# A branchformer forward and backward kernel: local steps paced by a VectorE budget, row scalings on ScalarE, conv weight gradient as tap products on TensorE

## The chip, the cores and the metric

One Trainium2 chip, one core of it. The metric is the device time of one execution, in microseconds, median over the runs of a job. A ratio is the mean time of one kernel's fast runs over that of the other's fast runs of the same rounds, so it is not quite the ratio of the medians quoted.

Words used throughout:

- A **unit** is a 1000-column piece of one 128-row block of the attention matrix. It has two **places** at which other work is put in. Four units are one row block, so eight places. A place is about 1.9 us here.
- The **local steps** are the work of the conv branch (GELU, layernorm, depthwise conv, their gradients), done for a **pair** of row blocks at a time and strewn over the places.
- A **conv** is the `pc` product group of a pair. Its channels 128 to 143 come as 80 rows (5 taps x 16 channels) through DRAM: a store to `gnC_d` (or `dgC_d` in the backward conv), then a load. This load is called the **gnC load** (or dgC load).

## The reference

```python
def _fwd_reference(x, w_qkv, w_att_out, w_mlp_in, dw_csgu, w_mlp_out, dw_merge, w_merge):
    B, T, D = x.shape                      # 2, 4000, 144; bf16; K = 5 taps
    xa = _layernorm(x)
    q, k, v = split(xa @ w_qkv)
    p = _softmax(q @ k.T * D ** -0.5)
    glob = (p @ v) @ w_att_out
    h = _gelu(xa @ w_mlp_in)
    u, g = h[..., :D], _layernorm(h[..., D:])
    gc = depthwise_conv(g, dw_csgu)        # gc[t] = sum_i g[t+i-2] * dw_csgu[i]
    loc = (u * gc) @ w_mlp_out
    m = concat(glob, loc);  m = m + depthwise_conv(m, dw_merge)
    return x + m @ w_merge
# the kernel returns this output and the gradients of all eight inputs for a given grad_out
```

The part that the change rebuilds is the gradient of `dw_csgu`: for each tap and channel, the sum over all tokens of `g` shifted by the tap, times the gradient that arrives at `gc`.

## The kernel before

For each of the two sequences there is a head, an attention stage with the local steps inside it, and a tail. The code of the attention stage that the change and the argument touch (cuts marked `# ...`):

```python
class Steps:                               # strews generators over the places
    def place(self, tensor=True):
        # all 'V' steps that are due (VectorE, ScalarE, GpSimd, DMA), as many as are ready
        # ... then at most one 'P' step (TensorE)

def pair(p):                               # local steps of row blocks 2p, 2p+1
    # ... GELU and layernorm give h_, gn, rs
    yield 'P', 2, aft(("gn", 1), ("ug", 2), ("wg", 4))
    gnC.put(p, gn)                         # 4 transposes, copies by ScalarE, store of 16 rows to gnC_d
    # ...
    yield 'V', 2                           # two places later
    gnC.fill(p)                            # the gnC load of pair p-1: 80 rows
    yield 'P', 4, ((("gn", min(p + 1, NPR - 1)), 6),) + aft(("ug", 1))   # four places after its load at the earliest
    pc = gnC.conv(p, False)                # last product of each block reads the 80 rows (w_c)
    # ... then the same with dgc through dgC.put, dgC.fill, dgC.conv

def wgrad(p):                              # gradient of dw_csgu, on VectorE
    yield 'V', 2, ((("dg", p), 2),)
    dgC.taps.spread(d8[0:80, :], p * 256, 256)
    for m in range(5):
        yield 'V', 1
        nc.vector.scalar_tensor_tensor(jg[:], a_[:, m:m + 256], 1.0, d_[:, 2:258], op0=ALU.mult, op1=ALU.mult, accum_out=dws[:, p, m:m + 1])
    # ... and one more for the 80 rows
for p in range(NPR):
    Q.add(14 * p, pair(p))
    Q.add(14 * p + 20, wgrad(p))

def row_end(i):                            # VectorE: sums, reciprocal rl, and
    nc.vector.tensor_scalar(Qs[:, pb, :], S.Q_t[:, i, :], rl[:], None, op0=ALU.mult)
    nc.vector.tensor_scalar(br[:], S.B_t[:, i, :], rl[:], None, op0=ALU.mult)
    nc.vector.scalar_tensor_tensor(Bt[:, pb, :], Qs[:, pb, :], nd[:], br[:], op0=ALU.mult, op1=ALU.add)

# a unit: pS and pD products; ScalarE: P = exp(pS); VectorE: Sm = pD * P; then
# y products (16 per unit) and X products (12 per fill); X is added into acc by VectorE, or ScalarE and GpSimd
ps_x = ps_f = Banks(pool, 3)               # three PSUM banks, shared by X and by all local steps
# all loads, stores and DMA transposes (PT, ST) of the stage are issued on SyncE's queue, in program order
```

## Time and profile before

| | before |
|---|---|
| time, median (lowest to highest), four runs | 1316.7 us (1311.2 to 1318.7) |
| profiled execution | 1318.5 us |
| TensorE / VectorE / ScalarE / GpSimd busy | 1222.5 / 986.3 / 806.0 / 580.4 us |
| the two attention stages, first `pS` to last `X` | 512.8 + 509.4 us |

The engines' line of the page of the kernel before:

```profile
PE 1222.5 (93%) x15116; PEld 957.1 (73%) x15116; DVE 986.3 (75%) x3421; ACT 806.0 (61%) x2370; POOL 580.4 (44%) x1033
```

The windows view of the kernel before, for its two attention stages (columns: the stretch, its length, busy time of each engine with the number of instructions, the granted TensorE clock, the mean busy share of the DMA engines, GB/s):

```profile
66.00:579.00 513.00, 489.55 (x5897) 369.71 (x5897) 407.62 (x1351) 328.51 (x986) 221.14 (x358) 0.99 0.87 152
...
696.00:1206.00 510.00, 488.36 (x5902) 369.56 (x5901) 407.60 (x1349) 328.37 (x987) 221.45 (x359) 0.99 0.88 151
```

TensorE is busy for 95% of these stages. That alone doesn't say that it streams at its peak. This case shows it in a striking way: the busy share is 93% before and 92% after a change that costs 35 us. So I read the distances between the starts of products. The timeline of the kernel before, TensorE:

```profile
401.09 1.16 PE L1903 MATMUL y<-ra,ST 128*128 128x144 bf16 x16
402.09 0.23 PE L1925 MATMUL X<-Qs,Sm 128*128 128x144 bf16 x1
```

Sixteen products of 144 columns take 1.00 us from start to start, 62.5 ns each. Products of 288 columns start 122 ns apart and those of 144 columns 62 ns (medians), so a column takes an estimated 0.416 ns, from these two, and some 2.5 ns a product are left. (Products of 128 columns start 56 ns apart, as this gives; those of 500 columns 215 ns, 4 ns more.) I used this as the time that a product needs and worked out, for every pair of successive products in the attention stages, what the distance holds beyond it. The rest goes to the wait that the profile names, or to a half-clock window (granted clock 0.5 in the record) if it lies in one, or to "small" (mostly a fixed 0.1 us where the array changes between 16-row and 128-row products: a 16-row product starts 158 ns after one of 144 columns, another of 144 columns 62 ns after it, medians):

| us, both attention stages | before | after |
|---|---|---|
| streaming, without the new products | 896.3 | 891.4 |
| the new tap products (`pw`) | - | 19.6 |
| small | 63.6 | 66.0 |
| waits for VectorE | 31.9 | 4.9 |
| waits for DMA | 10.8 | 40.0 |
| waits for ScalarE | 12.4 | 17.9 |
| lost to half clock | 7.2 | 23.6 |
| sum | 1022.2 | 1063.4 |

The waits of the whole kernel before, from the list of waits, TensorE (who waited for whom: us in all, times, longest):

```profile
PE X L1925 <- DVE acc L1939: 14.8, 16, 2.8
PE pc L1574 <- DMA gnC<-gnC_d: 9.1, 8, 2.1
...
PE pD L1854 <- DVE Sm L1868: 7.4, 26, 0.7
```

The groups that the change removes or moves, from the groups of the kernel before (busy us, mean ns | idle before):

```profile
L1785 DVE SCALAR_TENSOR_TENSOR jg<-gnC,dgC 128x256 bf16<-128x256 bf16 x160 | 92.0, 575 | 1.3
...
L1889 DVE TENSOR_SCALAR br<-B_t,rl 128x144 f32<-128x144 bf16 x64 | 18.5, 288 | 0.0
L1787 DVE SCALAR_TENSOR_TENSOR jg<-gnC,d 80x256 bf16<-80x256 bf16 x32 | 17.4, 545 | 0.0
L1887 DVE TENSOR_SCALAR Qs<-Q_t,rl 128x144 bf16<-128x144 bf16 x64 | 16.3, 254 | 0.0
```

### The profile page before, as it was taken

The numbers are of one execution on the slowest core, as the hardware profiler recorded it, in microseconds if no ns is written. First come the engines' busy times: TensorE is split into PE (matmuls) and PEld (weight loads), VectorE is DVE, ScalarE is ACT, GpSimd is POOL, SyncE is SP. The second block draws the span as 40 slices with busy tenths as digits, with TensorE's granted clock in tenths as the row PEclk, the third lists the DMA queues.
The fourth block names the chain that finished last, engine by engine and source line by source line (L and its number), as shares of the span: only waits on it lengthen the run. The fifth ranks groups of instructions, "written<-read, shape, count | busy, mean of one in ns | idle before, by whom it ended". The sixth has DMA issues, their size and how long they took to land. (4 is left out here: it accounts for less than half of the span.)

```text
span 1318.5 us, 39927 instructions
## 1 busy us (share of the span) xinstructions
PE 1222.5 (93%) x15116; PEld 957.1 (73%) x15116; DVE 986.3 (75%) x3421; ACT 806.0 (61%) x2370; POOL 580.4 (44%) x1033
## 2 busy tenths in 40 slices
PE   4899999999999999999989999999999999999986
PEld 2657776777777777798976677677777777779884
DVE  4666777887989888847735688788798888884664
ACT  2666666667667666546646666666766766654542
POOL 6312445444545454247611244545444544425640
PEclk9999999999999999999999999999999999999999
DMA  6369888887899889987775989888999988998851
GB/s 182 97 126 152 149 153 147 147 149 150 154 164 155 157 141 170 157 190 206 200 218 104 157 145 168 146 146 146 149 152 159 164 151 146 165 159 191 240 151 32
DMA packets 634223, 205.51 MB, mean 156 GB/s; under 512 B 577183, under 2 KB 631556, under 8 KB 633988
## 3 DMA queue, kind: packets, MB, share of 16 engines
q1 hardware_dynamic: 627472, 197.54, 79.3%
q10 hardware_dynamic: 6548, 5.33, 1.8%
q8 instruction: 120, 1.97, 0.6%
q14 instruction: 83, 0.68, 0.2%
HBM read 46.22 MB, written 21.79 MB: 52 GB/s over the span
## 5 line engine op out<-in xcount | busy, mean ns | idle before, releaser
L1868 DVE SCALAR_TENSOR_TENSOR Sm<-pD,Pm 128x500 bf16<-128x500 f32 x512 | 325.6, 673 | 104.0 <-PE pD L1858 71.4
L1866 ACT ACTIVATE Pm<-pS 128x500 bf16<-128x500 f32 x512 | 295.4, 584 | 99.6 <-PE pS L1858 96.8
L1925 PE MATMUL X<-Qs,Sm 128*128 128x144 bf16 x2048 | 286.5, 226 | 15.3 <-DVE acc L1939 14.8
L1937 POOL TENSOR_TENSOR acc<-xs,acc 128x432 f32<-128x432 f32 x150 | 172.3, 1148 | 268.3 <-ACT xs L1936 267.9
L1926 PE MATMUL X<-Bt,Pm 128*128 128x144 bf16 x2048 | 286.4, 226 | 0.8 <-DVE Bt L1890 0.8
L1926 PEld LDWEIGHTS <-Pm 128*128 128x128 bf16 x2048 | 200.6, 98 | 19.4 <-issue 18.4
L1925 PEld LDWEIGHTS <-Sm 128*128 128x128 bf16 x2048 | 200.5, 98 | 2.2 <-issue 1.0
L1903 PEld LDWEIGHTS <-ST 128*128 128x128 bf16 x2048 | 137.8, 98 | 28.2 <-issue 1.1
L1903 PEld LDWEIGHTS <-PT 128*128 128x128 bf16 x2048 | 137.4, 98 | 28.3 <-issue 0.5
L1936 ACT COPY xs<-X 128x432 f32<-128x432 f32 x150 | 77.7, 518 | 127.4 <-PE X L1926 113.9
L1939 DVE TENSOR_TENSOR acc<-X,acc 128x432 f32<-128x432 f32 x180 | 104.0, 578 | 65.6 <-PE X L1926 65.2
L1854 PE MATMUL pD<-rb,QBr 16*128 16x500 bf16 x448 | 100.8, 379 | 7.3 <-DVE Sm L1868 6.6
L1866 ACT ACTIVATION_READ_ACCUMULATOR Pm<-pS 128x1 f32 x512 | 103.3, 202 | 0.0
L1854 PE MATMUL pS<-rb,QBr 16*128 16x500 bf16 x448 | 92.4, 382 | 2.5 <-ACT Pm L1866 2.4
L1858 PEld LDWEIGHTS <-BTm 128*128 128x128 bf16 x512 | 50.0, 98 | 59.3 <-issue 1.5
L1785 DVE SCALAR_TENSOR_TENSOR jg<-gnC,dgC 128x256 bf16<-128x256 bf16 x160 | 92.0, 575 | 1.3
L1858 PEld LDWEIGHTS <-QTm 128*128 128x128 bf16 x512 | 29.1, 97 | 75.8 <-issue 75.8
L1913 POOL TENSOR_TENSOR B_t<-zd,yd 128x144 bf16<-128x144 f32 x64 | 34.3, 537 | 111.5 <-ACT zd L1912 111.5
L1892 POOL TENSOR_SCALAR nr<-nd,rl 128x1 f32<-128x1 f32 x64 | 20.5, 320 | 136.9 <-DVE nd L1886 136.7
L1858 PE MATMUL pS<-rb,QTm 128*128 128x500 bf16 x256 | 77.3, 384 | 0.0
L1858 PE MATMUL pS<-ra,QTm 128*128 128x500 bf16 x256 | 76.9, 382 | 0.0
L1858 PE MATMUL pD<-rb,BTm 128*128 128x500 bf16 x256 | 75.7, 377 | 0.0
(626 smaller groups left out, 2949.6 us busy)
## 6 DMA issues: line engine op xcount, KB each, us to landing
gs<-in_grad_out_dram SPq DMA_DIRECT2D x24, 720.0 KB
dh_d<-dh SPq DMA_DIRECT2D x32, 144.0 KB
dhr<-dh_d SPq DMA_DIRECT2D x16, 288.0 KB
gs<-in_grad_out_dram SPq DMA_DIRECT2D x8, 540.0 KB
xg<-in_x_dram SPq DMA_DIRECT2D x21, 144.0 KB
dug_d<-dug SPq DMA_DIRECT2D x16, 144.0 KB
dug<-dug_d SPq DMA_DIRECT2D x32, 72.0 KB
ug_d<-ug SPq DMA_DIRECT2D x32, 72.0 KB
```

The costliest lines, as they stand in the source:

```text
L1785: nc.vector.scalar_tensor_tensor(jg[:], a_[:, m:m + 256], 1.0, d_[:, 2:258], op0=ALU.mult, op1=ALU.mult, accum_out=dws[:, p, m:m + 1])
L1854: nc.tensor.matmul(o_[h][:, 0:SC], jt[i // 4][2][rr, i % 4, :], S.XR[c2][rr, 0:SC], start=True, stop=False)
L1858: nc.tensor.matmul(o_[h][:, 0:SC], jt[i // 4][w][:, i % 4, :], S.xaT[:, c0:c0 + SC], start=False, stop=True)
L1866: nc.scalar.activation(P[:, pb, c1:c1 + SC], o_[h][:, 0:SC], ACT.Exp, accum_out=ld8[:, 0, n_:n_ + 1])
L1868: nc.vector.scalar_tensor_tensor(Sm[:, pb, c1:c1 + SC], o_[h][:, 0:SC], 1.0, P[:, pb, c1:c1 + SC], op0=ALU.mult, op1=ALU.mult, accum_out=l ...
L1903: nc.tensor.matmul(y[:, w, :], src[:, jj, :], S.xaa[:, j, :], start=(j == 0), stop=(j == NBK - 1))
L1913: nc.gpsimd.tensor_tensor(S.Zn[:, i, :], zd[:], yd[:], op=ALU.add)
L1925: nc.tensor.matmul(X[:, jj, :], Sm[:, i % NP, j * 128:(j + 1) * 128], Qs[:, i % 4, :], start=(kk == 0 and jj == 0), stop=False, skip_group ...
L1926: nc.tensor.matmul(X[:, jj, :], P[:, i % NP, j * 128:(j + 1) * 128], Bt[:, i % 4, :], start=False, stop=(kk == 1), skip_group_check=True)
L1936: nc.scalar.copy(xs[:, 0:nj, :], X[:, 0:nj, :])
L1937: nc.gpsimd.tensor_tensor(a_, xs[:, 0:nj, :], a_, op=ALU.add)
L1939: nc.vector.tensor_tensor(a_, X[:, 0:nj, :], a_, op=ALU.add)
```

## The change

Its intent is to take work off VectorE and to even out the rest. The weight gradient becomes a token product on TensorE: `dgc` (tokens x channels, transposed as the weights) times the five tap-shifted copies of `gn`; the diagonal of each 128x128 result is what is wanted. The shifted copies are loaded from a new DRAM copy of `gn`, 720 KB for each group of four row blocks. The two row scalings of `row_end` go to ScalarE. VectorE steps get a cost, and a place admits them only within a budget of 1 (at most 1.3) per place; pairs start every 13.5 places. The first `X` fills move from a pair's last unit to the next pair's first. Some buffers shrink as well: `Rz`, an input of the first local products (`ph`), has one buffer instead of two.

```diff
+def gn_taps(k, dst, src, g, eng):
+    ap = bass.AP(tensor=src.tensor, offset=src[g * 512:g * 512 + 1, 0:1].offset, ap=[[D, 128], [128 * D, 4], [1, 5 * D]])
+    eng.dma_start(dst[:].rearrange("p j m c -> p j (m c)"), ap)
 # class Steps
-        return all(key in self.done and self.now >= self.done[key] + d for key, d in after)
+        return all(key in self.done and self.now >= self.done[key] + d for key, d in w[2]) and (w[3] == 0 or w[0] != 'V' or self.left >= w[3] / 2)
     def place(self, tensor=True):
+        self.left = min(self.left + self.rate, self.most)
 # ... _step takes the cost off self.left; steps are tried in the order in which they fall due
 # pair(p)
-        yield 'V', 2, aft(("dh", 6))
+        yield 'V', 2, aft(("dh", 6)), 1.2
 # ... and so for seven more steps
         gnC.put(p, gn)
+        nc.sync.dma_start(S.gn_d[2 + p * 256:2 + (p + 1) * 256, :].rearrange("(j p) c -> p j c", p=128), gn[:])
-    def wgrad(p):
 # ... all of it
+    def tapcorr(q):
+        yield 'V', 0, ((("gn", min(2 * q + 2, NPR - 1)), 2),) + (((("tap", q - 1), 0),) if q else ())
+        gtap = S.early.tile([128, 4, 5, D], BF, tag="gs", name="gtap")
+        gn_taps(k, gtap, S.gn_d, q, nc.sync)
+        for half in range(2):
+            yield 'L', 6 if half == 0 else 1, ((("dg", 2 * q + 1), 0),), .5
+            pw = ps.tile([128, 384], F32, tag="f", name="pw")
+            for j in range(4):
 # ... products of 384, or 256 and 80 columns
+            nc.vector.tensor_tensor(ds, pw[:, 0:w], ds, op=ALU.add)
-        Q.add(14 * p, pair(p))
+        Q.add(27 * p // 2, pair(p))
 # row_end
-            nc.vector.tensor_scalar(Qs[:, pb, :], S.Q_t[:, i, :], rl[:], None, op0=ALU.mult)
+            nc.scalar.activation(Qs[:, pb, :], S.Q_t[:, i, :], ACT.Copy, scale=rl[:])
-            nc.vector.tensor_scalar(br[:], S.B_t[:, i, :], rl[:], None, op0=ALU.mult)
+            nc.scalar.activation(br[:], S.B_t[:, i, :], ACT.Copy, scale=rl[:])
 # fills
-        fills = {(1, 0): ..., (7, 1): ((0, (0,)), (1, (0,)))}
+        fills = {(0, 1): ((0, (0,)), (1, (0,))), (1, 0): ..., (6, 1): ...}
-        Q = Steps()
+        Q = Steps(1, 1.3)
```

More of the change, by code (lines that the diff above doesn't have):

```diff
@@ L1520, in store @@
         (eng or self.nc.sync).dma_start(dst, src.unsqueeze(1).to_broadcast([DR, 5, w]))
-    def spread(self, dst, t0, w):
-        src = bass.AP(tensor=self.a.tensor, offset=self.a[2 * DR:2 * DR + 1, 2 + t0:3 + t0].offset, ap=[[0, 5], [self.L, DR], [1, w]])
-        self.nc.sync.dma_start(dst, src)
     def load(self, dst, t0, w, eng=None):
@@ L1535, in __init__ @@
         self.k, self.W, self.pool, self.ps, self.name = k, W, pool, ps, name
-        self.t, self.r, self.kept, self.kept8 = {}, {}, {}, {}
+        self.t, self.r = {}, {}
         self.taps = Taps(k, name + "_d")
@@ L1540, in put @@
         nc = self.k.nc
-        t = self.t[p] = self.kept[p] = self.pool.tile([128, 260], BF, tag=self.name, bufs=4, name=self.name)
+        t = self.t[p] = self.pool.tile([128, 260], BF, tag=self.name, bufs=3, name=self.name)
         r_ = self.pool.tile([128, 256], BF, tag=self.name + "s", bufs=2, name=self.name + "s")
@@ L1562, in fill @@
         for q in (p - 1, p)[0 if p else 1:2 if p == NBK // 2 - 1 else 1]:
-            r = self.r[q] = self.kept8[q] = self.pool.tile([128, 256], BF, tag=self.name + "8", bufs=4, name=self.name + "8")
+            r = self.r[q] = self.pool.tile([128, 256], BF, tag=self.name + "8", bufs=3, name=self.name + "8")
             self.taps.load(r[0:80, :], q * 256, 256)
@@ L1599, with __init__ @@
 class Steps:
-    def __init__(self):
+    def __init__(self, rate, most):
         self.now, self.done, self.tasks = 0, {}, []
+        self.left, self.rate, self.most = most, rate, most
     def add(self, at, gen):
@@ L1611, in mark, with use @@
         self.done[key] = self.now
+    def use(self, cost):
+        self.left -= cost
     def _ready(self, t):
@@ L1618, in _ready @@
             return True
-        kind, lag, after = w
-        return all(key in self.done and self.now >= self.done[key] + d for key, d in after)
+        return all(key in self.done and self.now >= self.done[key] + d for key, d in w[2]) and (w[3] == 0 or w[0] != 'V' or self.left >= w[3] / 2)
     def _step(self, t):
+        if t[1]:
+            self.left -= t[1][3]
         try:
@@ L1627, in _step @@
             return
-        w = (w + ((),))[:3] if len(w) < 3 else w
+        w = tuple(w) + ((), 0)[len(w) - 2:]
         t[0], t[1] = self.now + w[1], w
     def place(self, tensor=True):
+        self.left = min(self.left + self.rate, self.most)
         again = True
@@ L1635, in place @@
             again = False
-            for t in list(self.tasks):
+            for t in sorted(self.tasks, key=lambda t: t[0]):
                 if (t[1] is None or t[1][0] == 'V') and self._ready(t):
@@ L1654, in local_steps @@
     dgC = Chan(k, W, wk, ps, "dgC%d" % b)
-    dws = on.tile([128, NBK // 2, 5], F32, name="dws")
-    dw8 = on.tile([128, NBK // 2], F32, name="dw8")
-    jg = on.tile([128, 256], BF, name="jg")
-    Rz = [on.tile([128, 256], BF, name="Rz%d" % n) for n in range(2)]
-    for t in Rz:
-        nc.gpsimd.memset(t[:], 0.0)
+    dWs = on.tile([128, 5 * D], F32, name="dWs")
+    nc.gpsimd.memset(dWs[:], 0.0)
+    dgc_t = {}
+    jg = on.tile([128, D], BF, name="jg")
+    R = on.tile([128, 256], BF, name="Rz")
+    nc.gpsimd.memset(R[:], 0.0)
     def load_R(p):
-        nc.sync.dma_start(Rz[p % 2][112:128, :], S.R_d[:, p * 256:(p + 1) * 256])
+        nc.sync.dma_start(R[112:128, :], S.R_d[:, p * 256:(p + 1) * 256])
     load_R(0)
@@ L1672, in pair @@
         yield 'P', 0, aft(("z", 1), ("h", 2))
-        R = Rz[p % 2]
-        if p + 1 < NPR:
-            load_R(p + 1)
         hs = wk.tile([128, 2, 2 * D], BF, tag="hs", name="hs")
@@ L1686, in pair @@
             nc.scalar.activation(sq[:, j, :], ph[:], ACT.Square)
+        if p + 1 < NPR:
+            load_R(p + 1)
         yield 'V', 2, aft(("gp", 1))
@@ L1692, in pair @@
         nc.gpsimd.tensor_scalar(t3[:], sq[:], 6 * K0 * K1, 2 * K0, op0=ALU.mult, op1=ALU.add)
-        yield 'V', 2
+        yield 'V', 2, (), .5
         nc.vector.tensor_tensor(a_[:], a_[:], hs[:], op=ALU.mult)
@@ L1697, in pair @@
         nc.scalar.activation(a_[:], a_[:], ACT.Tanh)
-        yield 'V', 2, aft(("ug", 4))
+        yield 'V', 2, aft(("ug", 4)), .8
         h_ = wk.tile([128, 2, 2 * D], BF, tag="h_t", bufs=4, name="h_t")
@@ L1702, in pair @@
         Q.mark("h", p)
-        yield 'V', 1
+        yield 'V', 1, (), .95
         mv = sm.tile([128, 2, 2], F32, tag="mvg", name="mv")
@@ L1727, in pair @@
             nc.scalar.activation(gn[:, j, :], h_[:, j, D:2 * D], ACT.Identity, bias=nm[:, j:j + 1], scale=rs[:, j:j + 1])
-        yield 'P', 2, aft(("gn", 1), ("ug", 2), ("wg", 4))
+        yield 'P', 2, aft(("gn", 1), ("ug", 2))
         gnC.put(p, gn)
         Q.mark("gn", p)
+        nc.sync.dma_start(S.gn_d[2 + p * 256:2 + (p + 1) * 256, :].rearrange("(j p) c -> p j c", p=128), gn[:])
         dug = wk.tile([128, 2, D], BF, tag="dug", name="dug")
@@ L1734, in pair @@
         gnC.fill(p)
-        yield 'P', 4, ((("gn", min(p + 1, NPR - 1)), 6),) + aft(("ug", 1))
+        yield 'P', 4, ((("gn", min(p + 1, NPR - 1)), 6),) + aft(("ug", 1)) + (((("tap", p // 2 - 2), 0),) if p >= 4 else ())
         pc = gnC.conv(p, False)
@@ L1738, in pair @@
         nc.scalar.copy(gc[:], pc[:])
-        dgc = wk.tile([128, 2, D], BF, tag="dgc", bufs=2, name="dgc")
+        yield 'V', 0, (), .45
+        dgc = dgc_t[p] = wk.tile([128, 2, D], BF, tag="dgc", bufs=4, name="dgc")
         nc.vector.tensor_tensor(dgc[:], dug[:], h_[:, :, 0:D], op=ALU.mult)
-        yield 'V', 2, aft(("dh", 3))
+        yield 'V', 2, aft(("dh", 3)), 1.1
         dh = wk.tile([128, 2, 2 * D], BF, tag="dh", bufs=3, name="dh")
@@ L1749, in pair @@
         Q.mark("ug", p)
-        yield 'P', 1, aft(("dg", 1), ("dh", 3), ("wg", 4))
+        yield 'P', 1, aft(("dg", 1), ("dh", 3))
         dgC.put(p, dgc)
@@ L1760, in pair @@
             nc.scalar.activation(dg[:, q, :], pc[:, q, :], ACT.Copy, scale=rs[:, q:q + 1], accum_out=s12[:, 0, q:q + 1])
-        yield 'V', 2
-        jk = jg[:, 0:D]
+        yield 'V', 2, (), 1.1
+        jk = jg[:]
         for q in range(2):
@@ L1770, in pair @@
             nc.gpsimd.tensor_scalar(cc[:, q, :], gn[:, q, :], n12[:, 1, q:q + 1], n12[:, 0, q:q + 1], op0=ALU.mult, op1=ALU.add)
-        yield 'V', 2
+        yield 'V', 2, (), .75
         nc.vector.tensor_tensor(dg[:], dg[:], cc[:], op=ALU.add)
@@ L1775, in pair @@
         Q.mark("dh", p)
-    def wgrad(p):
-        yield 'V', 2, ((("dg", p), 2),)
-        d8 = wk.tile([128, 256], BF, tag="d8", bufs=2, name="d8")
-        dgC.taps.spread(d8[0:80, :], p * 256, 256)
-        a_, d_ = gnC.kept.pop(p), dgC.kept.pop(p)
-        for m in range(5):
-            yield 'V', 1
-            nc.vector.scalar_tensor_tensor(jg[:], a_[:, m:m + 256], 1.0, d_[:, 2:258], op0=ALU.mult, op1=ALU.mult, accum_out=dws[:, p, m:m + 1])
-        yield 'V', 1
-        nc.vector.scalar_tensor_tensor(jg[0:80, :], gnC.kept8.pop(p)[0:80, :], 1.0, d8[0:80, :], op0=ALU.mult, op1=ALU.mult, accum_out=dw8[0:80, p:p + 1])
-        dgC.kept8.pop(p, None)
-        Q.mark("wg", p)
@@ L1791, in ends @@
-    def ends():
-        yield 'V', 0, ((("wg", NPR - 1), 0),)
-        dc = sm.tile([128, 6], F32, tag="dc", name="dc")
-        nc.gpsimd.memset(dc[:], 0.0)
-        nc.vector.reduce_sum(dc[:, 0:5], dws[:].rearrange("p a m -> p m a"), axis=AX.X)
-        nc.vector.reduce_sum(dc[0:80, 5:6], dw8[0:80, :], axis=AX.X)
+    def tapcorr(q):
[6 more added lines that the diff above has]
+            for j in range(4):
+                d_ = dgc_t[2 * q + j // 2]
+                fl = dict(stop=(j == 3), skip_group_check=True)
+                if half == 0:
+                    nc.tensor.matmul(pw[:], d_[:, j % 2, 0:128], gtap[:, j, 0:3, 0:128], start=(j == 0), **fl)
+                else:
+                    nc.tensor.matmul(pw[:, 0:256], d_[:, j % 2, 0:128], gtap[:, j, 3:5, 0:128], start=(j == 0), **fl)
+                    nc.tensor.matmul(pw[:, 256:336], d_[:, j % 2, 16:D], gtap[:, j, :, 128:D], start=False, **fl)
+            w = 384 if half == 0 else 336
+            ds = dWs[:, half * 384:half * 384 + w]
+            nc.vector.tensor_tensor(ds, pw[:, 0:w], ds, op=ALU.add)
+        Q.mark("tap", q)
@@ new lines, in taps @@
+    def taps():
+        yield 'V', 0, ((("tap", NGR - 1), 0),)
+        dc = sm.tile([128, 2, 5], F32, tag="dc", name="dc")
+        jd = jg
+        for m in range(5):
+            nc.vector.scalar_tensor_tensor(jd[:, 0:128], dWs[:, m * 128:(m + 1) * 128], 1.0, id_[:], op0=ALU.mult, op1=ALU.mult, accum_out=dc[:, 0, m:m + 1])
+            nc.vector.scalar_tensor_tensor(jd[:, 0:DR], dWs[:, 640 + m * DR:640 + (m + 1) * DR], 1.0, id_[:, 112:128], op0=ALU.mult, op1=ALU.mult, accum_out=dc[:, 1, m:m + 1])
@@ L1797, in ends @@
         nc.vector.tensor_tensor(k.A.dwc[:], dc[:], k.A.dwc[:], op=ALU.add)
     for p in range(NPR):
-        Q.add(14 * p, pair(p))
-        Q.add(14 * p + 20, wgrad(p))
-    Q.add(0, ends())
+        Q.add(27 * p // 2, pair(p))
+    for q in range(NGR):
+        Q.add(27 * q + 20, tapcorr(q))
+    Q.add(0, taps())
 def phase_attn(k, W, b, S):
@@ L1886, in row_end @@
             nc.vector.tensor_scalar(nd[:], ld[:, 1:2], rl[:], -1.0, op0=ALU.mult, op1=ALU.mult)
-            nc.vector.tensor_scalar(Qs[:, pb, :], S.Q_t[:, i, :], rl[:], None, op0=ALU.mult)
+            nc.scalar.activation(Qs[:, pb, :], S.Q_t[:, i, :], ACT.Copy, scale=rl[:])
             br = sm.tile([128, D], F32, tag="br", bufs=2)
-            nc.vector.tensor_scalar(br[:], S.B_t[:, i, :], rl[:], None, op0=ALU.mult)
+            nc.scalar.activation(br[:], S.B_t[:, i, :], ACT.Copy, scale=rl[:])
+            Q.use(1)
             nc.vector.scalar_tensor_tensor(Bt[:, pb, :], Qs[:, pb, :], nd[:], br[:], op0=ALU.mult, op1=ALU.add)
@@ L1933, in xfill @@
                 (nc.scalar.copy if f % 2 else nc.vector.tensor_copy)(a_, X[:, 0:nj, :])
+                Q.use(0 if f % 2 else .6)
             elif f % 2 == 1:
@@ L1938, in xfill @@
             else:
+                Q.use(.6)
                 nc.vector.tensor_tensor(a_, X[:, 0:nj, :], a_, op=ALU.add)
-        fills = {(1, 0): ((0, (1,)), (1, (1,))), (1, 1): ((2, (0, 1)),), (2, 1): ((3, (0, 1)),), (3, 0): ((4, (0, 1)),), (3, 1): ((5, (0, 1)),),
-                 (4, 1): ((6, (0, 1)),), (5, 0): ((7, (0, 1)),), (5, 1): ((8, (0, 1)),), (6, 0): ((9, (0, 1)),), (6, 1): ((10, (0, 1)),), (7, 1): ((0, (0,)), (1, (0,)))}
-        Q = Steps()
+        fills = {(0, 1): ((0, (0,)), (1, (0,))), (1, 0): ((0, (1,)), (1, (1,))), (1, 1): ((2, (0, 1)),), (2, 1): ((3, (0, 1)),), (3, 0): ((4, (0, 1)),), (3, 1): ((5, (0, 1)),),
+                 (4, 1): ((6, (0, 1)),), (5, 0): ((7, (0, 1)),), (5, 1): ((8, (0, 1)),), (6, 0): ((9, (0, 1)),), (6, 1): ((10, (0, 1)),)}
+        Q = Steps(1, 1.3)
         local_steps(k, W, b, S, es, ps_f, Q)
@@ L1949, in phase_attn @@
             for i in range(NBK + 2):
+                if i == NBK:
+                    Q.rate = Q.most = 1.8
                 pr, half = i // 2 - 1, i % 2
@@ L1962, in phase_attn @@
                         for f, rows in fills.get((half * 4 + c2, place), ()):
-                            q = pr + 1 if rows == (0,) else pr
-                            if 0 <= q < NBK // 2:
-                                xfill(q, f, rows)
+                            if 0 <= pr < NBK // 2:
+                                xfill(pr, f, rows)
                         Q.place()
@@ L2241, in loads @@
             self.WoT, self.UT, self.U, self.WmT, self.Wqkv = self.F["WoT"], [self.F["UT0"], self.F["UT1"]], [self.F["U0"], self.F["U1"]], self.F["WmT"], self.F["Wqkv"]
-            self.dwcb = fp.tile([128, 6], BF, name="f_dwcb")
+            self.dwcb = fp.tile([128, 2, 5], BF, name="f_dwcb")
             nc.vector.tensor_copy(self.dwcb[:], A.dwc[:])
@@ L2276, in loads @@
             pt = self.T()
-            nc.tensor.transpose(pt[0:6, 0:128], self.dwcb[:], W.ident[:])
+            nc.tensor.transpose(pt[0:10, 0:128], self.dwcb[:].rearrange("p a b -> p (a b)"), W.ident[:])
             o = fp.tile([16, 128], BF, name="f_dwct")
-            nc.scalar.copy(o[0:6, :], pt[0:6, 0:128])
+            nc.scalar.copy(o[0:10, :], pt[0:10, 0:128])
             nc.sync.dma_start(self.k.out5[:, 0:128], o[0:5, :])
-            nc.sync.dma_start(self.k.out5[:, 128:D].unsqueeze(0), o[5:6, 0:80].rearrange("p (m r) -> p m r", r=DR))
+            nc.sync.dma_start(self.k.out5[:, 128:D], o[5:10, 112:128])
     def T(self):
@@ L2450, in bounded @@
         A.gr_d = tc.dram_tile([128, 4, D], F32, name="gr_d")
-        A.dwc = ap.tile([128, 6], F32, name="A_dwc2")
+        A.dwc = ap.tile([128, 2, 5], F32, name="A_dwc2")
         nc.vector.memset(A.dwc[:], 0.0)
@@ L2457, in bounded @@
             S.ug_d = tc.dram_tile([128, NBK, D], BF, name="ug_d%d" % b)
+            S.gn_d = tc.dram_tile([2 + NBK * 128 + 2, D], BF, name="gn_d%d" % b)
+            for r0 in (0, 2 + NBK * 128):
+                nc.sync.dma_start(S.gn_d[r0:r0 + 2, :].rearrange("a (b c) -> (a b) c", c=72), k.zero[0:4, :])
             S.R_d = tc.dram_tile([DR, NBK * 128], BF, name="R_d%d" % b)
```

## The prediction

> **What bounds the kernel.** TensorE. The page gives PE 1222.5 of 1318.5 us; in the two attention stages (about 66 to 562 and 722 to 1192 us) the windows view gives 917.9 of 961. A busy PE need not stream at its peak, so I read the timeline: the 16 `y` products of a unit take 1.00 us, 62.5 ns for 144 columns, and the `X` products behind them the same, back to back. [...] Taking that stream time off the distances between matmul starts leaves 59 and 52 us. About half is a fixed 0.1 us at changes of array tiling. Real waits are about 28 and 25 us: VectorE 31 together (in the list of waits `X` for `acc` 14.8, `pD` for `Sm` 7.4, and shorter ones), the DMA `gnC<-gnC_d` 9.1, ScalarE about 11. Three waits are followed by half-clock windows, some 5 us more. The local steps end inside the attention loop; nothing trails.
>
> **Removed and added.**
> - VectorE loses the 160 tap products (92.0 + 12.6 us with accumulator reads), the 32 on 80 rows (about 20), and `Qs` and `br` (16.3 + 18.5): 159 us. It gains 32 additions into `dWs`, estimated at 0.55 us from `acc` (0.60 us for 432 columns): 18 us. DVE 986 -> about 848.
> - ScalarE gains 128 scalings of 128x144, like `yd` (0.38 us): +40 to 48 us, 806 -> about 850. In attention it is about 65% busy and has room.
> - TensorE gains, per group of four blocks, 4 x (384 + 256 + 80) columns: by the rate above 1.3 to 1.5 us; 16 groups: +20 to 23 us, **all on the critical path**.
> - DMA gains 16 loads of 720 KB (8192 packets of 1440 B at 69 ns, as such packets take now: 35 us of 16 engines) and the `gn` stores, loses 32 spreads: share in attention about 0.88 -> 0.92. Order matters: each tap load goes out just ahead of a `gnC` load on the same queue, whose data the conv needs four places (7.5 us) later at the earliest. Today that lands 0.4 to 2.9 us before use. [...] then it lands an estimated 2 to 3.5 us later in 8 of 16 convs a batch: +5 to +12 us of PE waits. No trace shows it yet.
> - The budget, and the first `X` fills moved from the eighth unit into the next pair's first, take VectorE's bursts off the `X` banks and fill the short unit (2.3 us) where the row's end makes VectorE late.
>
> **Sum.** PE work +22; VectorE waits 31 -> about 8: -23; half clock -4; DMA waits +8; ScalarE +2; bank changes and pacing on waits counted as fixed -9: **1314 us**, range 1290 to 1338. Faster by over 2%: 0.10; within 2%: 0.82; slower: 0.08.
>
> **What would show each step.** DVE and ACT near 850, PE busy 1225 to 1245; 192 `pw` matmuls; PE's wait for `acc` below 4 us, for `Sm` below 3; for `gnC<-gnC_d` up from 9.1 to 12 to 25; DMA share up four points in attention; the head and the tails unchanged to 3 us.
>
> **What would make it wrong.** If the `gnC` loads aren't delayed and nearly all waits go, 1295. If they cause long waits with half clock, or ScalarE's later `Bt` holds up the `X` products, 1340.

## The result and the profile after

| | before | after |
|---|---|---|
| median (lowest to highest), four runs each | 1316.7 (1311.2 to 1318.7) | 1352.7 us (1349.7 to 1356.7) |
| ratio, 95% interval | | 1.0282 (1.0237 to 1.0328): slower |
| profiled execution, granted clock | 1318.5 us, 0.988 | 1353.1 us, 0.975 |
| TensorE / VectorE / ScalarE busy | 1222.5 / 986.3 / 806.0 | 1250.3 / 888.9 / 844.8 us |

The engines' line of the page of the changed kernel, and its windows over the two attention stages:

```profile
PE 1250.3 (92%) x15308; PEld 974.8 (72%) x15308; DVE 888.9 (66%) x2977; ACT 844.8 (62%) x2498; POOL 555.5 (41%) x1031
```

```profile
65.00:597.00 532.00, 502.29 (x5987) 378.13 (x5987) 358.51 (x1128) 347.76 (x1051) 209.95 (x360) 0.98 0.87 159
...
710.00:1242.00 532.00, 504.60 (x5993) 380.32 (x5991) 357.87 (x1126) 348.13 (x1052) 208.77 (x358) 0.97 0.87 159
```

VectorE did lose about 49 us in each attention stage (407.6 to 358.5), and yet each stage is 19 to 22 us longer. The DMA share did not rise: 0.87 and 0.88 before, 0.87 after. The whole loss of 34.6 us lies in the attention stages (+41.2); the rest of the kernel is 6.6 us shorter.

The waits of TensorE in the changed kernel:

```profile
PE pc L1576 <- DMA gnC<-gnC_d: 26.9, 13, 4.4
PE pc L1576 <- DMA dgC<-dgC_d: 8.4, 6, 2.2
...
PE X L1944 <- DVE acc L1960: 1.7, 2, 0.9
...
PE pD L1872 <- DVE Sm L1886: 1.5, 8, 0.2
```

The waits for VectorE are gone as intended (`acc` 14.8 to 1.7, `Sm` 7.4 to 1.5). In their place stand waits for the 80-row loads, 9.1 to 35.3 us. The granted clock of TensorE on the two pages (tenths of full speed in 40 equal slices of the execution; 8 means that part of the slice ran at half clock), first before, then after:

```profile
PEclk9999999999999999999999999999999999999999
```

```profile
PEclk8899999899999999999999999989999999999999
```

In the attention stages the half-clock windows add up to 15.4 us before and 49.9 us after; in them products of 144 columns start 120 ns apart (median), outside 62 ns. The new work, from the groups of the changed kernel:

```profile
L1798 PE MATMUL pw<-gtap,dgc 128*128 128x384 bf16 x64 | 13.0, 326 | 3.3 <-ACT dgC L1551 3.3
...
L1804 DVE TENSOR_TENSOR dWs<-pw,dWs 128x384 f32<-128x384 f32 (+1 forms) x32 | 16.9, 527 | 3.1 <-PE pw L1798 2.9
...
L1905 ACT ACTIVATE Qs<-Q_t,rl 128x144 bf16<-128x144 bf16 x64 | 26.6, 415 | 58.6 <-DVE rl L1902 58.6
L1907 ACT ACTIVATE br<-B_t,rl 128x144 f32<-128x144 bf16 x64 | 25.6, 400 | 0.0
```

Note the third line for later: ScalarE stood idle for 58.6 us in front of `Qs`, waiting for VectorE's reciprocal `rl`. A scaling took 0.25 and 0.29 us on VectorE and takes 0.42 and 0.40 us on ScalarE.

One bad wait in detail. SyncE's issues in the changed kernel (start, length of the issue):

```profile
328.30 0.74 SPq L1526 DMA_DIRECT2D gnC_d<-gnC0s  x1
...
329.56 0.46 SPq L1740 DMA_DIRECT2D dug<-dug_d  x1
331.99 0.37 SPq L1350 DMA_DIRECT2D gtap<-gn_d  x1
332.41 0.50 SPq L1529 DMA_DIRECT2D gnC<-gnC_d  x1
```

And TensorE at the same time:

```profile
332.18 0.44 PE L1575 MATMUL pc<-w_dg,gnC 128*128 128x128 bf16 x5
337.02 0.18 PE L1576 MATMUL pc<-w_c,gnC 80*128 80x16 bf16 x1 [4.40 <-DMA gnC<-gnC_d]
...
338.23 1.01 PE L1876 MATMUL pS<-rb,QTm 128*128 128x500 bf16 x2
```

The tap load of 720 KB goes out just ahead of the gnC load of 40 KB. The 80 packets of the gnC load end 3.50 us after its issue. TensorE, which had come to the 80-row product, waits 4.40 us. After that the record has a half-clock window from 337.1 to 340.5: two 500-column products take 1.01 us there, 0.60 us elsewhere. So this stall is paid again in what follows it.

Over all gnC loads in the changed kernel: the 16 that stand right behind a tap load land 3.64 us after their issue on average, the other 14 (of those whose order is comparable) 2.14 us; before, all 30 took 1.69 us.

### The profile page after: what moved, and what is told of

Same layout as the page of the kernel before. It is cut to its first block, busy times and chain, and to the rows that moved or that the text cites. A ratio compares the mean times of both kernels' runs of the same rounds, so it can differ in the third digit from the quotient of the medians.

```text
span 1353.1 us, 39968 instructions
## 1 busy us (share of the span) xinstructions
PE 1250.3 (92%) x15308; PEld 974.8 (72%) x15308; DVE 888.9 (66%) x2977; ACT 844.8 (62%) x2498; POOL 555.5 (41%) x1031
## 4 chain that ended last, share of the span: by engine, by line
PE 67%; DMA 11%; DVE 9%; ACT 5%; issue 3%; SPq 2%; POOL 2%; ACTq 0%; DVEq 0%; POOLq 0%
PE y L1922 15%; PE pS L1876 8%; PE X L1944 8%; PE X L1945 7%; PE pD L1876 7%; PE pS L1872 5%; DMA gnC<-gnC_d 4%; DVE Sm L1886 2%; PE pb L1473 2%; PE pc L1575 2%; PE po L2099 2%; SPq L1894 1%; DMA y<-r 1%; PE EF L2074 1%; PE gr L2170 1%
## 5 line engine op out<-in xcount | busy, mean ns | idle before, releaser
L1957 POOL TENSOR_TENSOR acc<-xs,acc 128x432 f32<-128x432 f32 x150 | 165.7, 1105 | 323.5 <-ACT xs L1956 323.0
L1922 PEld LDWEIGHTS <-PT 128*128 128x128 bf16 x2048 | 140.4, 99 | 30.5 <-issue 3.5
L1872 PE MATMUL pD<-rb,QBr 16*128 16x500 bf16 x448 | 93.2, 384 | 1.2 <-DVE Sm L1886 0.9
L1876 PE MATMUL pD<-ra,BTm 128*128 128x500 bf16 x256 | 77.6, 385 | 0.0
L1876 PEld LDWEIGHTS <-QTm 128*128 128x128 bf16 x512 | 29.2, 97 | 67.0 <-issue 67.0
L1922 PE MATMUL y<-rb,ST 128*128 128x144 bf16 x1024 | 76.9, 230 | 0.0
```

What stands on the lines that cost most here:

```text
L1872: nc.tensor.matmul(o_[h][:, 0:SC], jt[i // 4][2][rr, i % 4, :], S.XR[c2][rr, 0:SC], start=True, stop=False)
L1876: nc.tensor.matmul(o_[h][:, 0:SC], jt[i // 4][w][:, i % 4, :], S.xaT[:, c0:c0 + SC], start=False, stop=True)
L1922: nc.tensor.matmul(y[:, w, :], src[:, jj, :], S.xaa[:, j, :], start=(j == 0), stop=(j == NBK - 1))
L1957: nc.gpsimd.tensor_tensor(a_, xs[:, 0:nj, :], a_, op=ALU.add)
```

## The experiments

Theories after the result. **A**: the order. The tap load in front makes the gnC load late, the conv stalls, and the stall brings half-clock windows. **B**: the mere volume, 16 x 720 KB more. **C**: the pacing puts stores and loads at bad places between the DMA transposes. All times are with the kernel before in the same rounds. The ratios can be compared between jobs. The last column comes from one profiled execution, which is not the median one: in e11 and e12 it was the fastest (1338.9 and 1298.3 us), in e1, e8 and e10 the slowest (1341.3, 1334.3 and 1324.9 us).

| run | median | ratio to before (95%) | DMA / VectorE / ScalarE waits, half clock (us, attention, one profile) |
|---|---|---|---|
| the change | 1352.7 | 1.0282 (1.0237 to 1.0328) | 40.0 / 4.9 / 17.9, 23.6 |
| e1 load behind | 1335.1 | 1.0154 (1.0125 to 1.0183) | 30.0 / 4.9 / 18.9, 15.5 |
| e2 load once | 1323.6 | 1.0075 (1.0042 to 1.0108) | 18.8 / 4.9 / 18.9, 10.9 |
| e3 old pace | 1361.1 | 1.0353 (1.0321 to 1.0386) | 42.4 / 16.5 / 11.2, 24.4 |
| e8 ahead, wide | 1328.7 | 1.0086 (1.0041 to 1.0130) | 23.9 / 10.6 / 17.0, 18.7 |
| e4 behind, wide | 1311.1 | 0.9984 (0.9953 to 1.0016) | 8.0 / 10.4 / 17.4, 7.6 |
| e11 scalings back only | 1349.4 | 1.0282 (1.0255 to 1.0310) | 42.7 / 6.0 / 5.2, 13.5 |
| **e7 behind, wide, scalings back** | **1299.8** | **0.9881 (0.9840 to 0.9923)** | 7.3 / 11.6 / 5.9, 6.0 |
| e9 e7, load later still | 1300.3 | 0.9880 (0.9843 to 0.9916) | 5.8 / 12.0 / 5.9, 8.1 |
| e10 e7 with old pace | 1322.7 | 1.0050 (1.0016 to 1.0083) | 15.1 / 23.9 / 3.2, 8.3 |
| e12 e7 with old fills | 1303.2 | 0.9926 (0.9895 to 0.9956) | 3.9 / 14.6 / 11.1, 1.6 |
| e5 before, wide | 1319.8 | 1.0041 (1.0013 to 1.0069) | 1.5 / 35.8 / 14.8, 2.4 |
| e6 before, scalings on ScalarE | 1325.4 | 1.0084 (1.0053 to 1.0116) | 7.8 / 33.6 / 17.5, 8.2 |

### e1_load_behind

```diff
-        yield 'V', 0, ((("gn", min(2 * q + 2, NPR - 1)), 2),) + ...
+        yield 'V', 0, ((("gn", min(2 * q + 2, NPR - 1)), 3),) + ...
```

> The tap load goes out one place later, behind the gnC load of the same pair instead of ahead of it; nothing else differs from the changed kernel (1352.7 us, PE's wait for gnC<-gnC_d 26.9 us, for dgC<-dgC_d 8.4). Theory A (order on the queue: the 720 KB ahead of the gnC load make the conv late, and the stall brings half-clock windows): the gnC wait falls below 12 us, half-clock windows in the attention stages from about 50 to below 30 us, time 1325 to 1340. Rival B (the mere extra volume of DMA, in whatever order): gnC wait stays above 20, time 1348 to 1356. Rival C (the new pacing puts store and load at bad places between the transposes): the same as B, above 1345.

Measured: 1335.1 us. The gnC wait falls from 26.9 to 6.5 us. The same conv as above, SyncE's issues in this run:

```profile
328.28 0.72 SPq L1526 DMA_DIRECT2D gnC_d<-gnC0s  x1
...
331.97 0.32 SPq L1529 DMA_DIRECT2D gnC<-gnC_d  x1
332.33 0.43 SPq L1350 DMA_DIRECT2D gtap<-gn_d  x1
```

and TensorE:

```profile
332.18 0.44 PE L1575 MATMUL pc<-w_dg,gnC 128*128 128x128 bf16 x5
333.79 0.18 PE L1576 MATMUL pc<-w_c,gnC 80*128 80x16 bf16 x1 [1.17 <-DMA gnC<-gnC_d]
```

Up to here the two kernels run alike to 0.02 us. Only the two loads are exchanged: the 80 packets now end 1.49 us after their issue, not 3.50, and the stall is 1.17 us, not 4.40. This shows A for the gnC load. The packets of the change agree: the 512 of the tap load run from 333.02 to 335.78 us, the 80 of the gnC load from 335.21 to 335.90. The half-clock windows fall from 49.9 to 34.1 us, a little above what I expected. B and C as I had stated them (above 1345 us) are refused. But the exchange takes away less than half of the loss: the ratio is still 1.0154, some 20 us, and the dgC wait has grown from 8.4 to 16.3 us:

```profile
PE pc L1576 <- DMA dgC<-dgC_d: 16.3, 10, 3.2
...
PE pc L1576 <- DMA gnC<-gnC_d: 6.5, 5, 1.8
```

Only two of its 30 dgC loads went out within 2 us behind a tap load, so I don't claim that the moved load explains all of this growth. Another 4.2 us of e1's DMA waits are a single wait for the load of `Rz` at the start of the first attention stage (3.9 in e3, 4.0 in e8, 1.1 in the change, 0.2 before); it has nothing to do with the order.

### e2_load_once

```diff
-        gtap = S.early.tile([128, 4, 5, D], BF, tag="gs", name="gtap")
-        gn_taps(k, gtap, S.gn_d, q, nc.sync)
+        if q == 0:
+            dgc_t["once"] = S.early.tile([128, 4, 5, D], BF, tag="gs", name="gtap")
+            gn_taps(k, dgc_t["once"], S.gn_d, q, nc.sync)
+        gtap = dgc_t["once"]
```

> The tap load is done only for the first group of each batch and its data used for all (wrong conv weight gradient on purpose); tensor and vector work unchanged. A and B both: gnC wait to 5 to 12 us, time 1315 to 1335; under A it is no more than about 8 us faster than the run with the load behind, under B at least 20 us faster. C: DMA waits of PE stay above 25 us in all, time above 1340.

The result is wrong in the one conv weight gradient. Measured: 1323.6 us, gnC wait 9.8, dgC 5.2. It is 11.4 us faster than e1, between what A (8 at most) and B (20 at least) allowed, so neither forecast held. With 2 of the 16 tap loads left, the DMA waits of both attention stages are still 18.8 us, against 10.8 before, so a part of the loss doesn't come from the loads.

### e3_old_pace

```diff
-        Q = Steps(1, 1.3)
+        Q = Steps(1000, 1000)
-        Q.add(27 * p // 2, pair(p))
+        Q.add(14 * p, pair(p))
# and the groups of tap products every 28 places instead of 27
```

> The changed kernel without the budget and with the old distance of pairs (14 places); tap products, scalings and moved fills kept. C: PE's DMA waits fall from 35 to below 15 us, VectorE waits stay below 15 because 140 us of VectorE work is gone, time 1325 to 1338. A and B: gnC wait stays above 18 us (the load is still ahead of it), only the dgC wait goes; time 1340 to 1356.

Measured: 1361.1 us, slower than either theory allowed. The gnC wait is even larger (34.5 us), the dgC wait nearly gone. So the pacing is not the cause of the gnC waits, but it is where the 8.4 us of dgC waits come from: C is right for that part. Also, the waits for VectorE stay at 16.5 us here, half of those before. With the loads repaired, but also without the pacing, 23.9 us are left (e10), so 16.5 may be too favourable; that VectorE catches up during the long DMA stalls of e3 would explain it, but was not tested. The pacing removes most of the rest.

### e4_behind_wide

```diff
# e1, and
-        yield 'P', 4, ((("gn", min(p + 1, NPR - 1)), 6),) + ...      # gnC.conv
+        yield 'P', 6, ((("gn", min(p + 1, NPR - 1)), 8),) + ...
-        yield 'P', 4, ((("dg", min(p + 1, NPR - 1)), 6),) + aft(("dh", 1))   # dgC.conv
+        yield 'P', 6, ((("dg", min(p + 1, NPR - 1)), 8),) + aft(("dh", 1))
```

> The tap load behind the gnC load, and both convs two places later after their loads (six instead of four). If late landings are the whole loss (A, with C for the dgC part): PE's DMA waits below 5 us, half-clock windows in attention below 20 us, time 1300 to 1318, perhaps a little under the kernel before. If volume is the cause (B): 1335 or more.

Measured: 1311.1 us, ratio 0.9984: the whole loss is gone. DMA waits 8.0 us (a little more than expected), half-clock windows 16.2 us long instead of 49.9. The mean slack between the landing of a gnC load and its use is 4.57 us, 1.42 before. The tap loads still move every byte, and the DMA share is 0.92 to 0.93. B is refused: the volume alone isn't the cause. (With little slack the mere presence of the loads still costs something, see e1 and e2.)

### e8_ahead_wide

```diff
# the two wide convs of e4 alone; the tap load stays ahead
```

> The changed kernel with nothing but both convs two places (about 3.8 us) later after their loads; the tap load stays ahead of the gnC load. Theory A (a load that lands about 2 us late is the loss, not its volume and not the order as such): with 3.8 us more slack PE's wait for gnC falls from 26.9 below 4 us, dgC below 5, half-clock windows in attention from about 50 below 20 us, time 1305 to 1320, within 8 us of the run with the load behind and wide convs (1311.1). Rival: if the order costs something besides the landing (the transposes behind the tap load), it stays above 1322.

Measured: 1328.7 us, and 16.0 us of waits for gnC. This missed; the slack alone doesn't do it, and the bound of the rival (1322) is passed. From the waits of TensorE in this run:

```profile
PE pc L1576 <- DMA gnC<-gnC_d: 16.0, 7, 4.0
```

In e4, which differs from e8 in the order alone, TensorE waits for no gnC load in the attention stages. I compare load by load the 14 gnC loads that stand behind a tap load here with the same 14 in e4, where they stand ahead of it. They are issued 7.59 us after their store (e4: 6.79) and land 3.52 us after that (e4: 1.91). The 3.52 is a lower bound: a dgC load of equal packets often follows at once. So being behind costs at least 1.6 us of landing and 0.8 us of issue. The time between the last packet and TensorE's coming to the product falls from 3.17 to 0.82 us on average.

The added slack was also smaller than I had reckoned. The product comes about 3.6 us later after the store than in the change, but the load is issued 2.1 us later as well (5.50 to 7.59). That is not the order: from e1 to e4, with the tap load behind, it also came later (4.84 to 6.79). Without the pacing it is issued after 3.64 us (e10; e7: 6.68), so the pacing has a part in it; why the wide convs bring it out is not shown.

### e5_before_wide

```diff
# the kernel before, with the two wide convs
```

> The kernel before with the same two places more for both convs: is the repair a gain of the change or one that the old kernel could have had? PE's DMA wait 9 -> below 2 us, half clock perhaps a window fewer; 1298 to 1310. If it is at or below the repaired change (1311.1), the tap products gain nothing even when their load is harmless: PE +20 us eats what VectorE gives. Rival (the change is good once repaired): it stays at 1311 or above.

Measured: 1319.8 us, ratio 1.0041. This missed: the DMA waits do go (1.5 us), but the waits for VectorE rise to 35.8. What is repaired in one wait seems to come up in another as long as VectorE is full. So the old kernel did not gain from the repair, and the rival reading (the change is good once repaired) holds. That a full VectorE is the reason is my reading of one profile, not a test.

### e6_before_scal

```diff
# the kernel before, with only Qs and br as nc.scalar.activation(..., ACT.Copy, scale=rl[:])
```

> The kernel before with only the two row scalings moved from VectorE to ScalarE. ACT +50 us busy, DVE -35, PE's waits for acc and Sm 22 -> 12 to 18 us; the Bt that comes later waits for at most 2 us in all. 1306 to 1314, that is same to 0.5% faster. Rival: ScalarE's longer row end holds up the X products or the exp, time above 1316.

Measured: 1325.4 us, ratio 1.0084, and the waits for VectorE unchanged (33.6). This missed. The part of the change that I had taken for nearly free costs 10 us alone and relieves nothing.

### e7_wide_vscal

```diff
# e4, with Qs and br back on nc.vector.tensor_scalar
```

> The tap load behind and wide convs (1311.1), but the two row scalings back on VectorE. If the scalings on ScalarE cost waits (PE waits for ACT copies of gc and dgC, some 13 us in that run): 1302 to 1309. If they relieve VectorE: 1312 to 1320, with PE's waits for acc and Sm up from 8 to above 13 us.

Measured: **1299.8 us, ratio 0.9881**, and correct: 1.2% faster than the kernel before. The interval lies below 1. Against e4 (0.9984) the scalings are worth 1.0%, and the two intervals don't overlap. ScalarE waits fall from 17.4 to 5.9 us while those for VectorE rise by only 1.2. Why, the trace of e4 shows. ScalarE in e4:

```profile
246.33 0.25 ACT L1884 ACTIVATION_READ_ACCUMULATOR Pm<-pS 128x1 f32 x1
248.83 0.41 ACT L1905 ACTIVATE Qs<-Q_t,rl 128x144 bf16<-128x144 bf16 x1 [2.25 <-DVE rl L1902]
...
250.25 0.38 ACT L1746 CAST gc<-pc 128x288 bf16<-128x288 f32 x1
```

TensorE in e4:

```profile
246.85 0.17 PE L1576 MATMUL pc<-w_c,gnC 80*128 80x16 bf16 x1
...
250.67 0.28 PE L1688 MATMUL ph<-w_i,rb 128*128 128x288 bf16 x1 [2.89 <-ACT gc L1746]
```

ScalarE takes these instructions in the order of the program. `Qs` waits 2.25 us for the reciprocal that VectorE computes only after the row's last `Sm` (248.63, after 247.71). The copy `gc` that would free a PSUM bank was ready at about 247.0, while ScalarE stood idle, but stands behind it (and behind `br` and two writes of `gn`) and begins at 250.25, and TensorE wants that bank for `ph`: 2.89 us of stall, followed by a half-clock window at 252. On VectorE the same scaling waits for nothing (idle time 0.0 in front of `Qs` in the groups of the kernel before): it comes after the reciprocal on the same engine.

### e11_vscal_only

```diff
# the changed kernel, with Qs and br back on nc.vector.tensor_scalar
```

> The changed kernel (1352.7 us) with only the two row scalings back on VectorE; tap load still ahead, convs still four places after. Theory: on ScalarE the scalings make its in-order queue wait for VectorE's reciprocal (58.6 us of ScalarE idle in the trace of the change), so the copies that free PSUM banks come late; PE's waits for ACT (about 12 us in the two stages) fall below 6, time 1340 to 1348. Rival (their 11 us in the repaired kernel came from a lucky order of the loads there): 1350 or more.

Measured: 1349.4 us, ratio 1.0282, the same as the change. Six runs spread from 1338.9 to 1353.1 us: two near 1339, four from 1348.8 on. The profile is of the fastest. In it the ScalarE waits do fall, from 17.9 to 5.2, and the half-clock loss from 23.6 to 13.5, while the DMA waits stay (42.7); and this one execution is 16 us shorter than the profiled one of the change. Of the four slower ones there is no profile. As long as the loads are late, this part can't be told from the spread: inconclusive for the time. With the loads repaired it is worth 1.0% (e4 to e7).

### e9_clear

```diff
# e7, with the tap load at lag 5 instead of 3
```

> The best so far (tap load behind, wide convs, scalings on VectorE: 1299.8 us) with the tap load two places later still, where by the program's order no dgC load goes out in the three places after it (before: right after it in five of eight groups of a batch). If it is the order that counts: PE's wait for dgC 4.8 -> below 2 us, time 1293 to 1299. If not, 1300 or more.

Measured: 1300.3 us; the dgC wait 3.7 us, not below 2. No gain over e7. The order right at the dgC loads is not what is left.

### e10_vscal_old_pace

```diff
# e7, with Steps(1000, 1000), pairs every 14 places, tap products every 28
```

> The same best version without the budget, pairs 14 places apart again: what is the pacing worth once the loads do no harm? If it keeps VectorE's bursts off the PSUM banks: PE's waits for acc and Sm from 10 to 18 us or more, time 1305 to 1315. If the removed VectorE work alone does it: within 4 us of 1299.8.

Measured: 1322.7 us, ratio 1.0050, 1.7% slower than e7 and worse than I expected. The waits for VectorE double to 23.9 us, and `y` now waits for a transpose:

```profile
PE X L1944 <- DVE acc L1960: 9.5, 8, 1.5
...
PE y L1922 <- DMA PT<-Pm: 6.4, 2, 3.5
```

So the pacing is needed for the gain. Whether the tap products are needed too is open: the pacing was never run with the VectorE sums. Tap products without it (e10, 1.0050) are no better than VectorE sums without it and with the same wide convs (e5, 1.0041).

### e12_old_fills

```diff
# e7, with the first X fills back in the eighth unit
```

> The same best version with the first X fills back in the eighth unit. If the move matters: PE's waits for acc and Sm up by 5 us or more, time 1303 to 1312. If not: within 4 us of 1299.8.

Measured: 1303.2 us, ratio 0.9926; the interval (0.9895 to 0.9956) overlaps that of e7. The move of the fills is worth at most a few microseconds; not settled.

## Why the prediction was wrong

Point by point, with the two attention stages of the profile:

| step of the sum | predicted | measured |
|---|---|---|
| tap products on TensorE | +22 | +19.6 |
| waits for VectorE | -23 | -27.0 |
| half clock | -4 | **+16.4** |
| DMA waits | +8 | **+29.2** |
| ScalarE | +2 | +5.5 |
| pacing and bank changes on small gaps | -9 | +2.4 small, -4.9 streaming |
| rest of the kernel | 0 | -6.6 |
| sum | about -4 | +34.6 |

Two steps failed: the half-clock term, in its sign, and the step from a late load to a wait, in its size. The prediction had named this case ("If they cause long waits with half clock", 1340) but gave slower a chance of 0.08.

- **Right:** what bounds the kernel, the cost of the tap products, and the removal of the VectorE waits. (The bounds that it gives for the stages are too narrow: in the trace they run from 66 to 579 and from 696 to 1206 us.) ScalarE's 844.8 us is as predicted. VectorE's busy time is not: predicted 848, measured 888.9 us. Its records, added up, fall from 1169.4 to 1035.1 us, 134 less, not far from the 141 that I subtracted (159 off, 18 on). But on VectorE the record of one instruction often begins before that of the one before it ends, and busy time counts such an overlap once: 183.1 us of overlap before (1169.4 less 986.3), 146.2 after. So the instructions taken out took less off the busy time (97.4 us) than their records are long.
- **Right in mechanism, wrong in size:** the DMA waits. The prediction wrote: "then it lands an estimated 2 to 3.5 us later in 8 of 16 convs a batch: +5 to +12 us of PE waits." That a load behind the tap load has to wait for it was my assumption; of the estimate, 2.2 us follow from the 35 us for 16 tap loads. The loads behind a tap load do land about 2 us later (1.69 to 3.64 us after issue). The term measured +29.2 us in the attention stages: gnC 9.1 to 26.9 us, and 8.4 us of dgC that I did not foresee at all and that the pacing brings (e3). What was wrong is how much of a delay becomes a wait. I had let most of it be hidden. The 14 loads compared in e8 had on average 1.03 us between their last packet and TensorE's coming to the product before. After the change they land 2.0 us later (1.69 to 3.72 us after issue), and that time is -0.90 us: TensorE waits 25.0 us for them instead of 6.1. Sixteen loads that are 2 us late with 1 us to spare already give an estimated 16 us (from these numbers), not 5 to 12; and a stalled product began another 0.5 to 1.2 us after the last packet.
- **The step that failed in sign:** "half clock -4". I took the half-clock windows of the trace before as a handful that would go with the VectorE waits. The new DMA stalls are longer than the VectorE waits they replace, and here the length counted: in the attention stages there were four stalls of TensorE of 1.5 us or more before (two for gnC loads, two for VectorE) and 13 after (eight for gnC, two for dgC, three for ScalarE). A half-clock window began in or within 2 us after 3 of the four and 10 of the 13, and after none of the 47 stalls of 0.6 to 1.5 us in the two traces. The half-clock loss rose from 7.2 to 23.6 us.
- **A cost that I called room:** "In attention it is about 65% busy and has room." ScalarE has room on average, but the moved scaling waits there for VectorE (58.6 us of idle ScalarE in front of `Qs` in the change), and in e4 the copy `gc` behind it, ready at about 247.0, began at 250.25. e6 shows +0.8% for it alone, e4 to e7 1.0%.
- **The DMA share** was predicted to rise by four points. It stayed at 0.87 in the slow change and is 0.94 to 0.95 in the repaired e7. The share of a stage that is longer is no measure of the load in it.

What stays open: why the dgC wait grew in e1; whether the moved fills matter (e12); what the tap products are worth apart from the pacing; why the loads are issued later with wide convs (e8); and why four of e11's six runs are as slow as the change. e5 is slower by its runs (1.0041) though its profiled execution is 3.7 us shorter than that of before; with one profile each I don't explain it further.

## What to carry to other kernels

When a large load is put on a queue that also carries small loads with little slack, issue it behind them, and give the small ones more slack; look at landing against use, not at the share of DMA time. (Here the 40 KB load landed 3.50 us after its issue behind the 720 KB load, 1.49 us ahead of it.) Long stalls of TensorE were paid more than once here because of the half clock after them: over all traces here the half-clock loss came to 156 us, against 253 us of stalls of 1.5 us or more. So a change that trades many short waits for a few long ones can lose, as this one did (1.0282). Before moving an instruction to an engine with free time, ask what it waits for there, and what stands behind it: on ScalarE in e4 the copy `gc`, which frees a PSUM bank, began 3.2 us after it was ready.

## What the traces showed of the hardware

- Half clock after stalls of TensorE. Over the 14 traces, in the attention stages, a half-clock window began in or within 2 us after a stall in 0 of 240 stalls of 0.6 to 1.5 us, 13 of 37 of 1.5 to 2, 17 of 21 of 2 to 2.5, 25 of 28 of 2.5 to 3, and 16 of 17 above; 71 of the 78 windows that began in these stages began so. Windows lasted 3.4 or 6.8 us.
- Order on the queue. Here an 80-packet load of 40 KB ended 1.49 us after its issue in front of a 720 KB load (e1) and 3.50 us behind it (the change); and with wide convs the same 14 loads were issued 7.59 us after their store with the large load ahead in SyncE's program order (e8), 6.79 us with it behind (e4).
- Scalings. The scaling of 128x144 by a per-partition scale took 415 ns (bf16 out) and 400 ns (f32 out) on ScalarE after the change, 254 and 288 ns on VectorE before.
- A scaling in front of a copy. In e4 2.25 us of wait on ScalarE became 2.89 us of stall on TensorE, because the copy that frees a PSUM bank stood behind the scaling.
